# A four-layer attention kernel on one core: a new issue order, with key-value sums spread, the last key block in halves, and halo copies on GpSimd

## The chip, the core and the metric

The kernel runs on one core of a Trainium2 chip. A core has a matrix engine (TensorE, PE in the profile; its weight loads are listed as PEld), a vector engine (VectorE, DVE), a scalar engine (ScalarE, ACT), a general engine (GpSimd, POOL) and an engine that here only issues transfers (SyncE, SP). Each engine takes its instructions in the order of its own queue and waits on semaphores for the others. Data lies in SBUF, matrix products land in PSUM in eight banks of 128x512 fp32.

The metric is the device time of one execution in microseconds. Five runs of the kernel before gave a median of 334.54 us, from 333.26 to 336.47.

## The reference

Four layers, A, B, A, B, on x of 2048 rows by 512, 32 heads of 16. Each adds its result to x after a layer norm.

```python
def _A_ref(x, wqkv, w_phi, wo):
    pq = einsum("bhsd,hdf->bhsf", q, w_phi)          # the same for k
    phi_q = concatenate([softmax(pq), softmax(-pq)])  # the same for k
    kv = einsum("bhsf,bhsd->bhfd", phi_k, v)
    z  = einsum("bhsf->bhf", phi_k)
    o = einsum("bhqf,bhfd->bhqd", phi_q, kv) / (einsum("bhqf,bhf->bhq", phi_q, z) + 1e-6)
    return o @ wo
def _B_ref(x, wqkv, wo):
    # each row attends to 8 rows of its own past, 2 apart
    logits = einsum("bhsd,bhswd->bhsw", q, kg) * scale   # masked before row 0
    o = einsum("bhsw,bhswd->bhsd", softmax(logits), vg)
    return o @ wo
x = x + _A_ref(ln(x)); x = x + _B_ref(ln(x)); x = x + _A_ref(ln(x)); x = x + _B_ref(ln(x))
```

## The kernel before

The 2048 rows are four blocks (0 to 3) of 512; L is 0 for the first A and B layer and 1 for the second pair. Work is cut into steps, and a step issues a few instructions on one engine. The stages, with their lines in the profile:

- `s_a1` (A layer, keys and values of a block): projections L575 and L587, two exponentials of the keys on ACT L581, a tree of additions over 16 features on DVE L608 to L621 for four tiles at a time, the reciprocal on ACT L627 and L628, the normalising multiply on DVE L633, and the key-value sums L650. One sum step is for one tile of 128 rows: 16 small matmuls of 64 columns that add to one PSUM bank for the whole layer. Sixteen such steps make a layer's sums.
- `s_a2` (queries): projection L680, exponentials L688, their sums L696, logarithm and exponential for the reciprocal L702 and L703.
- `s_akv`: when all sums are in, eviction (through the helper `copy`: L184 is DVE, L186 is ACT), four transposes L726, and the masked copies ZM and R, L735 and L739. Nothing of `s_a3` can start earlier.
- `s_a3`: denominators L764, L772, L775, L778, L779, L783. Then, for blocks 0 and 1, the factor is spread over partitions by small matmuls L790 and multiplied into the query features on DVE straight from PSUM, L796. Blocks 2 and 3 go by way of DRAM, L803 and L810, with the multiply L814.
- `s_a4`: outputs L855, then `s_out`: output projection L511, the residual either as one more matmul L514 with an eviction on ACT L521, or as an addition on DVE L524; the squares L531 and `s_norm` for the next layer (L421 to L460), with transposes on PE (L453) or by a transfer (L444).
- `s_b1` (B layer): projections L879 of Q, K and V. K and V have 16 columns of halo in front: the last 16 columns of the block before. K's are copied on DVE (L905), V's go out to a small tile and in again on ACT (L921, L917). Block 0 has zeros, written by POOL (L909, L913). V is then copied by transfers on SP (L931) into Vg, in shifted form, 16 transfers per block.
- `s_b2`: products of queries and windows of keys on DVE, L960, one per quarter; sums of them by L967; exponentials L974, denominators L983, L988, L990, and probabilities L995.
- `s_b3`: products with the values on DVE L1020, summed by L1027, evicted by `copy`, and `s_out` again. In the last layer, `s_out` stores x (L535).
- `s_flag`: a check that no sum overflowed (L1048 to L1065); each engine loads the flag (L1072) and branches on it to a general version of the kernel, or past it.

The order is written out by hand. `_ORDER` is a list of base-36 numbers; each names one list of steps of a stage on one engine, and issues the next step of it. The queues of PE, DVE, ACT and SP follow this order, while POOL was left to the recording layer. `_CHOICE` has a digit for every step that may run on DVE (1) or ACT (0), and `_SLOTS` the buffer of each tile, for `big`, `med`, `t2` and PSUM tiles. A tile waits for the last reader of the tile that had its buffer.

## Time and profile before

| | us |
|---|---|
| median of the runs | 334.54 |
| the profiled execution | 332.56 |
| its span, first to last instruction | 330.8 |
| PEld busy | 149.8 |
| ACT busy | 281.2 |
| POOL busy | 5.8 |
| key-value sums L650, 512 matmuls, busy | 8.3 |
| L960, 32 instructions on DVE, busy | 72.2 |
| L1020, 32 instructions on DVE, busy | 71.7 |

Busy time of an engine is the time covered by its instructions; a matmul's end is modelled, so PE's is an upper value. In a line of the timeline stand the start, the time covered, the engine, the line of the kernel, the operation, output and inputs, shapes, and the count; the bracket gives the idle time of the engine just before and what ended it. "issue" is time in which the engine waited for nothing that the profile shows. The clock that was granted to PE was 0.995 of full speed over the execution.

### The profile page before, as it was taken

The page shows a single profiled execution, that of the slowest core. Times are in us where ns is not written, and L with a number is a line of the kernel's source. Part 1 is how long each engine was busy: PE and PEld are TensorE (multiplying, and loading weights), DVE is VectorE, ACT ScalarE, POOL GpSimd, SP SyncE. Part 2 cuts the span into 40 slices and gives each one's busy share as a digit, 9 for nine tenths or more (in the row PEclk, how much of TensorE's full clock was granted, in tenths as well). Part 3 has the DMA queues.
Part 4 walks back from the last instruction along what each step waited for, and adds up shares of the span by engine and source line. Part 5 has one row for each costly group of instructions (what it writes and reads, how often), then busy time and mean ns, then how long its engine had stood idle before and what let it go on. Part 6 is the DMA issues. An engine that isn't in the chain of part 4 may idle for free.

```text
span 330.8 us, 7975 instructions
## 1 busy us (share of the span) xinstructions
PE 310.8 (94%) x3189; PEld 149.8 (45%) x3189; DVE 300.4 (91%) x422; ACT 281.2 (85%) x644; POOL 5.8 (2%) x32
## 2 busy tenths in 40 slices
PE   8999997999999999999999999789999999997883
PEld 4645446545444444444444455643544444442321
DVE  4899995798899899999999999498999999999993
ACT  4999996899998898999999999788799998685630
POOL 4000000000000000000000000000000000000000
PEclk9999999999999999999999999999999999999997
DMA  7980000004399999794990300013469988689915
GB/s 211 322 232 3 0 0 4 4 14 124 80 157 112 181 132 173 126 141 105 159 133 13 63 1 2 4 40 101 108 91 159 123 162 157 139 142 155 186 54 168
DMA packets 37325, 35.42 MB, mean 107 GB/s; under 512 B 22944, under 2 KB 32160, under 8 KB 37280
## 3 DMA queue, kind: packets, MB, share of 16 engines
q1 hardware_dynamic: 36752, 34.81, 56.2%
q8 instruction: 27, 0.44, 0.6%
q14 instruction: 18, 0.15, 0.2%
q10 hardware_dynamic: 528, 0.02, 0.1%
HBM read 10.50 MB, written 2.36 MB: 39 GB/s over the span
## 4 chain that ended last, share of the span: by engine, by line
PE 66%; DVE 13%; ACT 11%; DMA 4%; issue 3%; SPq 0%; DVEq 0%; ACTq 0%
PE ps L879 19%; PE ps L511 13%; PE ps L575 6%; PE ps L587 6%; PE ps L680 5%; DMA xnT<-xn 4%; PE ps L967 3%; DVE Eq L796 3%; DVE prod L960 3%; PE ps L1027 3%; ACT oT L186 2%; DVE Ek L633 2%; PE ps L281 2%; ACT sqd L531 2%; PE ps L453 2%
## 5 line engine op out<-in xcount | busy, mean ns | idle before, releaser
L879 PE MATMUL ps<-xnT,WB 128*128 128x512 bf16 x384 | 88.5, 380 | 1.2 <-ACT V L186 0.7
L960 DVE TENSOR_TENSOR prod<-QT,K 128x4096 bf16<-128x4096 bf16 x32 | 72.2, 2287 | 1.1 <-ACT K L186 0.9
L1020 DVE TENSOR_TENSOR pav<-PT,Vg 128x4096 bf16<-128x4096 bf16 x32 | 71.7, 2288 | 0.9 <-PE ps L967 0.4
L879 PEld LDWEIGHTS <-WB 128*128 128x128 bf16 x384 | 42.2, 114 | 44.8 <-issue 7.8
L511 PEld LDWEIGHTS <-oT 128*128 128x128 bf16 x256 | 23.7, 98 | 31.9 <-ACT oT L186 4.1
L186 ACT CAST oT<-ps 128x512 bf16<-128x512 f32 x57 | 31.4, 603 | 6.4 <-PE ps L1027 5.3
L688 ACT ACTIVATE Eq<-ps 128x512 bf16<-128x512 f32 x64 | 35.0, 614 | 1.2 <-PE ps L680 1.1
L581 ACT ACTIVATE Ek<-ps 128x512 bf16<-128x512 f32 x64 | 34.2, 628 | 0.0
L511 PE MATMUL ps<-WoA,oT 128*128 128x512 bf16 x128 | 31.2, 380 | 1.4 <-ACT oT L186 1.4
L680 PE MATMUL ps<-xnT,WA 128*128 128x512 bf16 x128 | 31.0, 380 | 1.0 <-issue 0.8
L511 PE MATMUL ps<-WoB,oT 128*128 128x512 bf16 x128 | 31.5, 379 | 0.0
L587 PE MATMUL ps<-WA,xnT 128*128 128x512 bf16 x128 | 30.7, 379 | 0.0
L575 PE MATMUL ps<-WA,xnT 128*128 128x512 bf16 x128 | 30.0, 379 | 0.4 <-DMA xnT<-xn 0.4
L531 ACT ACTIVATE sqd<-x 128x512 bf16<-128x512 bf16 x48 | 30.0, 635 | 0.3
L524 DVE SCALAR_TENSOR_TENSOR x<-ps,x 128x512 bf16<-128x512 f32 x36 | 23.5, 686 | 1.0 <-PE ps L511 0.6
L521 ACT ACTIVATE x<-ps 128x512 bf16<-128x512 f32 x28 | 16.4, 597 | 8.0 <-PE ps L514 7.6
L439 ACT ACTIVATE xn<-x,nmr,rstd 128x512 bf16<-128x512 bf16 x27 | 21.4, 821 | 2.0 <-DVE nmr L428 2.0
L186 ACT CAST QT<-ps 128x512 bf16<-128x512 f32 x30 | 17.3, 593 | 3.6 <-issue 2.5
L796 DVE TENSOR_TENSOR Eq<-ps,Eq 128x512 bf16<-128x512 f32 x32 | 19.8, 684 | 0.1
L186 ACT CAST V<-ps 128x512 bf16<-128x512 f32 x31 | 17.5, 602 | 2.4 <-PE ps L879 2.4
L186 ACT CAST K<-ps 128x512 bf16<-128x512 f32 x30 | 17.7, 595 | 2.1 <-PE ps L879 1.8
L1027 PE MATMUL ps<-pav,indAV 128*32 128x512 bf16 x256 | 17.0, 382 | 2.6 <-DVE pav L1020 2.6
(126 smaller groups left out, 406.9 us busy)
## 6 DMA issues: line engine op xcount, KB each, us to landing
Vg<-V SPq DMA_DIRECT2D x128, 131.5 KB, 4.8
Prho<-rd SPq DMA_DIRECT2D x8, 512.0 KB
out_dram<-x SPq DMA_DIRECT2D x8, 256.0 KB, 3.9
x<-in_A_x_dram SPq DMA_DIRECT2D x3, 512.0 KB, 7.1
WB<-in_B_wqkv_dram SPq DMA_DIRECT2D x3, 512.0 KB, 10.3
wraw<-in_A_wqkv_dram SPq DMA_DIRECT2D x4, 256.0 KB
x<-in_A_x_dram SPq DMA_DIRECT2D x4, 128.0 KB, 4.4
WA<-in_A_wqkv_dram SPq DMA_DIRECT2D x1, 512.0 KB
```

The source lines that it names most:

```text
L186: self.nc.scalar.copy(out=out, in_=in_)
L511: nc.tensor.matmul(y[:], lhsT=oT[:, c, t * P:(t + 1) * P], rhs=Wo()[:, c, :], start=(c == 0), stop=(c == NB - 1 and not onpe))
L531: nc.scalar.activation(out=sqd[:], in_=xb[:, t, :], func=ACT.Square, accum_out=T["ss"][:, t:t + 1])
L575: nc.tensor.matmul(pk[:], lhsT=xnT[:, t, k, :], rhs=self.WA[:, k, D:2 * D], start=(k == 0), stop=(k == NB - 1))
L581: nc.scalar.activation(out=T["E"][:, t, s, :], in_=T["k", t][:], func=ACT.Exp, scale=1.0 - 2.0 * s)
L587: nc.tensor.matmul(pv[:], lhsT=xnT[:, t, k, :], rhs=self.WA[:, k, 2 * D:3 * D], start=(k == 0), stop=(k == NB - 1))
L680: nc.tensor.matmul(pq[:], lhsT=self.WA[:, k, hb * P:(hb + 1) * P], rhs=xnT[:, :, k, :], start=(k == 0), stop=(k == NB - 1))
L688: nc.scalar.activation(out=self.Eq[L, b][s][:, :, hb, :], in_=T[hb][:].rearrange("p (t i) -> p t i", t=4), func=ACT.Exp, scale=1.0 - 2.0 * s)
L796: nc.vector.tensor_tensor(out=ev, in0=T["pb", s][t][:].rearrange("p (a i) -> p a i", a=NB), in1=ev, op=ALU.mult)
L879: nc.tensor.matmul(pp[:], lhsT=self.WB[:, k, i * D + c:(i + 1) * D:NB], rhs=xnT[:, :, k, :], start=(k == 0), stop=(k == NB - 1))
L960: nc.vector.tensor_tensor(out=pr[:], in0=QT[:, c:c + 1, :].to_broadcast([P, NW, TB]), in1=win, op=ALU.mult)
L1020: nc.vector.tensor_tensor(out=pv[:], in0=PT[:].unsqueeze(1).to_broadcast([P, NB, 2, TB]), in1=vw, op=ALU.mult)
```

## The change

The order, the choices and the slots are replaced as a whole. In the new order the key-value sums of a layer no longer stand in one run: in layer 0 eight steps, then four value projections, then the other eight; in layer 1 eight steps, then seven projections, then the other eight. The feature normalisation of key block 3 is issued for two tiles at a time (`half_k`). The halo copies go to POOL, and POOL's queue now follows the order as well. The eviction of the products from PSUM in `s_a3` becomes a choice for each tile: multiplied straight from PSUM, or copied to SBUF by ACT first (7 of 32 are). The eviction of the key-value sums is on DVE. The load of the flag may be issued within the order, 12 steps after the flag is computed; nine steps follow that point in the new order. `split`, which would cut the last steps in two, is empty.

```diff
 _OPT = {
-    "rho_act": (),
-    "half_k": (),
+    "half_k": ((0, 3), (1, 3)),
     "half_ln": (),
+    "split": (),
     "warm": 14,
+    "flag_lag": 12,
 }
-_ORDERED = {_E.PE, _E.DVE, _E.Activation, _E.SP}
+_ORDERED = {_E.PE, _E.DVE, _E.Activation, _E.SP, _E.Pool}
 _ORDER = """
-0 0 0 8 i 9 i i i i i i i i i i i i i 2t j o k j l a b p 3 3 o q 1x 1x 1z 27 r s 2 1q 1y 1x 1x 20 t 1r 0 t 1x
...
+d5 0 bh 4i 9 8 i i i i i i i a i i i 0 i i i i 0 d f g c j k o p j 3 t l h 1x 3 1x 0 2 o 2i q r b t m n 1y 1q
...
-        def mulp(s, t):
+        def mulp(s, t, direct):
             ev = self.Eq[L, b][s][:, t, :, :]
-            nc.vector.tensor_tensor(out=ev, in0=T["pb", s][t][:].rearrange("p (a i) -> p a i", a=NB), in1=ev,
-                                    op=ALU.mult)
+            src = T["pb", s][t] if direct else T["bs", s, t]
+            nc.vector.tensor_tensor(out=ev, in0=src[:].rearrange("p (a i) -> p a i", a=NB), in1=ev, op=ALU.mult)
...
-        def bev(s, t, dve):
...
+        def bev(s, t, direct):
+            if direct:
+                self.slot("t2")
+            else:
+                T["bs", s, t] = self.t2([TB], "bs")
+                nc.scalar.copy(out=T["bs", s, t][:], in_=T["pb", s][t][:])
...
-            nc.vector.tensor_copy(out=self.K[L, b][:, :, 0:16], in_=self.K[L, b - 1][:, :, TB:KVW])
+            nc.gpsimd.tensor_copy(out=self.K[L, b][:, :, 0:16], in_=self.K[L, b - 1][:, :, TB:KVW])
...
-            nc.scalar.copy(out=T["V"][:, :, 0:16], in_=self.vh[L, b - 1][:])
+            nc.gpsimd.tensor_copy(out=T["V"][:, :, 0:16], in_=self.vh[L, b - 1][:])
...
-            nc.scalar.copy(out=self.vh[L, b][:], in_=T["V"][:, :, TB:KVW])
+            nc.gpsimd.tensor_copy(out=self.vh[L, b][:], in_=T["V"][:, :, TB:KVW])
...
-            add(st + "v", "ACT", vhalo_in)
+            add(st + "v", "POOL", vhalo_in)
...
-            add(st + "k", "DVE", halo)
+            add(st + "kh", "POOL", halo)
         if b < 3:
-            add(st + "v", "ACT", vhalo_out)
+            add(st + "v", "POOL", vhalo_out)
...
         for w in _ORDER.split():
             key = self.names[int(w, 36)]
             i = n.get(key, 0)
             n[key] = i + 1
             self.threads[key][i]()
+            if key == "flag.DVE" and i == 1:
+                left = _OPT["flag_lag"]
+            if left is not None:
+                left -= 1
+                if left == 0:
+                    self.redo = self.flag()
+        if left is None or left > 0:
+            self.redo = self.flag()
...
-        redo = fast.flag()
+        redo = fast.redo
```

The amounts of work change little: VectorE issues 405 instructions up to the flag in place of 394, ScalarE 547 in place of 555, TensorE one matmul less, GpSimd 18 copies more.

## The prediction

> **What bounds the kernel now.** I read the busy shares first, then busy time by stretch of the span, then the order of time inside the stretches that have idle time.

> ```profile
> PE 310.8 (94%) x3189; PEld 149.8 (45%) x3189; DVE 300.4 (91%) x422; ACT 281.2 (85%) x644; POOL 5.8 (2%) x32
> ```

> ```profile
> 50.00:68.00 18.00, 15.64 (x557) 10.16 (x556) 12.65 (x28) 13.53 (x31) 0.54 (x2) 1.00 0.01 4
> ...
> 208.00:224.00 16.00, 12.96 (x435) 7.60 (x427) 11.31 (x26) 12.50 (x29) 0.00 (x0) 1.00 0.11 27
> ```

> ```profile
> 215.65:320.24 104.59, 97.47 (x873) 44.28 (x876) 102.23 (x109) 83.65 (x199) 0.15 (x1) 1.00 0.71 128
> 61.44:206.35 144.91, 143.67 (x1211) 66.16 (x1211) 138.75 (x188) 137.63 (x324) 1.46 (x5) 1.00 0.60 98
> ```

> The columns after the length are busy us of PE, weight loads, DVE, ACT and POOL. Four parts show. From 61 to 206 us PE is the bound (143.67 of 144.91 busy). From 215.65, where the last layer's feature products begin, to 320.24, where the last attention product ends, DVE is the bound (102.23 of 104.59). After 320.24 a tail runs out. Between lie two hand-overs, at the end of the key-value sums of each layer (50 to 61, 206 to 216), in which every engine idles: in the windows around them PE idles 2.36 and 3.04 us, DVE 5.35 and 4.69. A gain must come out of these two, the tail, or DVE's queue after 215.65; more work for ACT or POOL costs nothing by itself.

> ```profile
> 50.30 2.91 PE L650 MATMUL ps<-Ek,vaug 128*33 128x64 bf16 x176
> 54.40 1.35 PE L650 MATMUL ps<-Ek,vaug 128*33 128x64 bf16 x80 [1.20 <-issue]
> 55.68 0.63 PE L696 MATMUL ps<-Eq,indS 128*32 128x128 bf16 x32
> 56.42 0.40 PE L726 MATMUL ps<-ident,kvT 128*128 128x128 bf16 x4
> 56.75 0.35 PE L696 MATMUL ps<-Eq,indS 128*32 128x128 bf16 x12
> 57.85 0.46 PE L696 MATMUL ps<-Eq,indS 128*32 128x128 bf16 x20 [0.75 <-issue]
> ```

> ```profile
> 209.74 0.29 PE L696 MATMUL ps<-Eq,indS 128*32 128x128 bf16 x6
> 210.95 0.57 PE L696 MATMUL ps<-Eq,indS 128*32 128x128 bf16 x26 [0.93 <-issue]
> ...
> 214.68 0.60 PE L680 MATMUL ps<-xnT,WA 128*128 128x512 bf16 x2 [0.84 <-issue]
> ```

> Four times PE stops with no engine to wait for: 1.20, 0.75, 0.93 and 0.84 us, 3.72 together. Count between the stops: 80+32+4+12 = 128 matmuls in layer 0, 26+4+32+64+2 = 128 in layer 1 (the rows between are the transposes and L696, L764). With a weight load each that is 256 instructions. In 50 to 60 us the transfers hold one queue alone, three packets of some 16 KB:

> ```profile
> q8 instruction: 3, 0.05, 1.9%
> ```

> So PE takes in instructions in blocks of 256, and a new block was there 54.40 to 57.85 = 3.45 us after the one before, or 210.95 to 214.68 = 3.73. 128 pairs of L650 take 128 x 16.3 ns (8.3 us over 512) = 2.1 us and run dry; 128 matmuls of 512 columns take 27 us and never do.

> [...]

> **The change, part by part.** All steps are made against the profiled execution, 332.56 us, of which the span is 330.8. The shown runs have median 334.54; I take the difference over to it unchanged.

> 1. *Layer 0, sums spread.* Decoded, the new PE order is: eight key-value steps of 16 matmuls, four value projections (16 x 216 ns = 3.5 us), four steps, four steps, a Q projection (0.86), the transposes, a Q projection, then denominators (32 small), sums (32), denominators (32), a Q projection. Cut in blocks of 128 from the same count (the start has as many), the shortest holds 3.9 us of work (104 x 16.3 ns, 16 small, 8 x 216), above 3.45. Both stops should go: -1.95. The Q projection before the transposes covers the eviction of the sums (0.58 on ACT before, 0.69 on DVE now). Of PE's idle 2.36 I take **-2.2**. PE bounds what follows, so all of it counts.

> 2. *Last key block in halves* (L608 to L633 for block 3). DVE work: the four-tile multiply is 2.287, halves are 2 x 1.22 (the 128x2048 row L814), tree and reciprocal halves add about 0.3 a level by the next smaller rows: +1.6 a layer, ACT +0.35. That lies where PE is the bound and DVE has 144.91 - 138.75 = 6.2 us free. In return, only two sum steps (32 x 16.3 = 0.5) instead of four (1.1) follow the last multiply: -0.6 on the chain.

> 3. *Layer 1 hand-over.* Before: the last multiply ends at 208.64, the first product L796 begins at 215.65, 7.0 us. After, link by link with the durations of that stretch: two sum steps 0.6, L696 0.72 (covers the eviction), transposes 0.46, the other L696 0.72 (covers L735 and L739), L764 0.6, L772/775 0.75, L778/779 0.8, L783 0.45, L790 0.46: 5.6. Stops come on top. One block of 128 still has only 2.1 us of work and the next 3.5, but steps in the first wait for the two last multiplies anyway. Between no stop (-1.4) and both (+0.4) I choose 0.4 us of stops: **-1.0**.

> 4. *After the first product of layer 1 (DVE).* Ahead of the last product L1020: three more residual adds (3 x 0.69), three K halos less (3 x 0.176), four L796 products from SBUF in place of PSUM (0.684 to 0.425, the same shape in bf16, L616): +2.06 - 0.53 - 1.04 = +0.5. The four take ACT 4 x 0.6, which has 20.9 us free here. Three more of them in layer 0 are hidden likewise; they put an ACT link before a product, but other products are queued between.

> 5. *Tail.*

> ```profile
> 306.94 13.30 DVE L1020 TENSOR_TENSOR pav<-PT,Vg 128x4096 bf16<-128x4096 bf16 x6
> ...
> 325.13 0.69 DVE L524 SCALAR_TENSOR_TENSOR x<-ps,x 128x512 bf16<-128x512 f32 x1 [0.30 <-PE ps L511]
> ```

> From 320.24 to 325.82 is 5.58. Before, L1027 for the last two products ran together after PE had finished an output projection, and one projection adds x on PE. New: L1027 0.66, eviction 0.63, the 13 matmuls left (13 x 0.216 + 0.16 = 2.97), add 0.74: 5.0, so -0.6. With part 4: **-0.1**. The 5.0 us from 325.82 to 330.8 stay: store, its landing (3.9 median), the closing barrier.

> 6. *Flag register.* The load is put 12 steps after the flag is known, but only nine steps follow in the new order, so it is issued at the end: in each engine's queue it stays last. **0**: that part does not do what it says.

> 7. *Halos on POOL.* 18 copies leave ACT (12 x 0.26, not the bound) and DVE (counted). A K halo waits for ACT's evictions of the earlier block; the first L960 of the block waits for it. A V halo stands before 16 Vg copies on SP (131.5 KB, 4.8 us to land each), behind which normalised transposes queue. The trace has no POOL copy. Nearest rows: POOL's memset of the same 128x64 shape, 0.15 (L913), and of a strided one, 0.39 to 0.48 (L596). [...] I take **+0.4**, nearer the rows; ends 0 and 4.3.

> 8. *Start and the rest of the order.* Both evictions of the first folded weight are now on ACT (1.0 each, one was 0.69 on DVE): **+0.3**, ends 0 and 0.6. DVE's named waits after 215.65 sum to 1.6 (L428 0.6, L543 0.5, L524 0.3, L960 0.2); the new order has large products queued ahead of some: **-0.3**, ends +0.5 and -1.6. PE's two waits for transposed x (0.47, 0.43) may stay or go.

> Sum: -2.2 - 1.0 - 0.1 + 0.4 + 0.3 - 0.3 = -2.9: 329.7 for the profiled execution, **331.6** for the median.

> **Rivals.**
> (a) *The waits elsewhere shrink too*: both transposed-x waits (0.9), DVE's 1.6 and all stops of layer 1 (0.4) go, POOL costs nothing (0.4): about 3 more, 328.6. For it: the order is new everywhere. Against: PE and DVE have under 2% idle there. Chance 0.22.
> (b) *The gain is not collected*: stops move to layer 1 (+1.4 against my choice) and DVE's queue takes back 0.8: 333.8, no measurable change. For it: the short block of 2.1 us. Chance 0.13.
> [...] Chance 0.08.
> My forecast has 0.57.

> **Numbers.** Range 328.0 to 335.2: it takes in (a) for the most part, (b), and my own -1.5 to -5 from the bounds above, and leaves out most of (c). 0.5% (1.67 us) is about what can be told from no change here. Faster: 0.57 less a little, (a), a little of (b): 0.79; same 0.13; slower 0.08.

> **What will show it.** Right: no issue stop over 0.3 us at layer 0's key-value sums, first L796 of layer 1 near 212 to 213 us, register loads last on every queue, DVE still full from there to the last L1020, and under 5.2 us from it to the last add. Wrong: stops inside the spread sums; POOL copies lasting over 0.5 us or DVE gaps of that size beside them; PE idle between 61 and 206 us that makes up for layer 0; or a later first L796 although the stops are gone.

## The result and the profile after

Timed side by side on the same chip, the changed kernel took 332.51 us (median of 26, 330.60 to 335.75) and the kernel before 334.4 us. The ratio is 0.9939, with a 95% interval from 0.9923 to 0.9956: about 2.0 us less. The ratios leave out slow executions, one of the 26 here, and so differ a little from the ratio of the medians. A second series of the same pair gave 0.9951 (0.9927 to 0.9976). So the change is a gain, within the range, and about two thirds of the 2.9 us that the forecast summed up.

The profiled execution took 331.27 us with a span of 329.55 (332.56 and 330.84 before), 1.29 us less. The busy shares show nothing of it:

```profile
PE 311.5 (95%) x3188; PEld 150.6 (46%) x3188; DVE 302.1 (92%) x435; ACT 278.7 (85%) x634; POOL 28.4 (9%) x50
```

DVE has 1.7 us more work and POOL 22.6 more. The windows of the two hand-overs, and then the two long stretches between the marks of the prediction (columns as there):

```profile
50.00:68.00 18.00, 17.20 (x431) 9.59 (x429) 14.14 (x29) 15.67 (x36) 0.00 (x0) 1.00 0.02 4
208.00:224.00 16.00, 14.07 (x355) 7.24 (x353) 14.03 (x32) 14.60 (x36) 0.00 (x0) 1.00 0.24 64
```

```profile
211.93:319.29 107.36, 99.12 (x875) 45.21 (x874) 103.10 (x111) 84.84 (x193) 12.56 (x9) 0.98 0.79 129
58.62:206.32 147.70, 146.88 (x1384) 69.57 (x1384) 141.00 (x191) 137.43 (x323) 10.57 (x12) 1.00 0.51 96
```

PE's idle time fell from 2.36 to 0.80 us and from 3.04 to 1.93 in the hand-overs. In the last stretch, DVE's work grew from 102.23 to 103.10 us and its idle time from 2.36 to 4.26. Cut at the same marks, the two executions read (in us):

| stretch | before | after | predicted change | measured |
|---|---|---|---|---|
| to the first product of layer 0, L796, now L812 | 61.44 | 58.62 | -1.9 | -2.82 |
| to the last multiply of layer 1's keys, L633, now L647 | 147.20 | 147.70 | 0 | +0.50 |
| hand-over to the first L812 of layer 1 | 7.01 | 5.61 | -1.0 | -1.40 |
| to the last product with the values, L1020, now L1036 | 104.59 | 107.36 | +0.6 | +2.77 |
| tail, to the last addition to x, L524, now L529 | 5.58 | 5.44 | -0.6 | -0.14 |
| to the end of the span | 5.02 | 4.82 | 0 | -0.20 |

The rows add up to the 1.29 us between these two executions, not to the 2.0 us between the medians; 0.7 us of the gain stands in no trace.

Both hand-overs gave more than predicted. One stretch gave 2.8 us back, and not all along: from the first product of layer 1's B layer (L960, now L974) to the last L1036 both kernels take 79.3 us. The loss lies in the 28.11 us before that product (25.31 before).

The sums themselves, on PE's timeline, in layer 0 and then in layer 1:

```profile
45.27 2.05 PE L664 MATMUL ps<-Ek,vaug 128*33 128x64 bf16 x128
47.25 3.63 PE L601 MATMUL ps<-WA,xnT 128*128 128x512 bf16 x16
50.81 2.19 PE L664 MATMUL ps<-Ek,vaug 128*33 128x64 bf16 x128
...
205.00 2.05 PE L664 MATMUL ps<-Ek,vaug 128*33 128x64 bf16 x128
...
207.83 0.40 PE L740 MATMUL ps<-ident,kvT 128*128 128x128 bf16 x4 [0.23 <-DVE kvT L187]
```

No stop by issue is left in either hand-over: four stops of 3.72 us are gone. But PE's timeline has one in a new place, and DVE's, below it, is held by it:

```profile
223.97 0.39 PE L516 MATMUL ps<-WoA,oT 128*128 128x512 bf16 x1
225.97 1.67 PE L516 MATMUL ps<-WoA,oT 128*128 128x512 bf16 x7 [1.61 <-issue]
```

```profile
224.75 0.41 DVE L797 TENSOR_TENSOR rho<-rS,Ds 128x256 bf16<-128x256 f32 x1
226.81 0.69 DVE L529 SCALAR_TENSOR_TENSOR x<-ps,x 128x512 bf16<-128x512 f32 x1 [1.64 <-PE ps L516]
```

Counted in PE's instructions, the place lies a whole number of blocks (16 x 256) behind the place of the 1.20 us stop of the kernel before. But PE took 7.5 and 6.0 us for the two blocks ahead of it (210.5 to 218.0 and 218.0 to 224.0 us), more than the 3.45 to 3.73 us in which a block arrived. Small matmuls alone don't explain it. The transfers do more: PE passed the place before, at 217.99 us, and the queue's own timeline has the broadcast reads of block 2 issued just ahead of that:

```profile
215.87 1.38 SPq L825 DMA_DIRECT2D Prho<-rd  x2
```

All that moved from 218.3 to 223.2 us, and then from 223.2 to 224.6 (queue, packets, MB, share of the transfer engines):

```profile
q1 hardware_dynamic: 162, 0.63, 48.3%
```

```profile
q1 hardware_dynamic: 41, 0.17, 47.7%
q8 instruction: 1, 0.02, 5.6%
```

For five microseconds only the two reads of 512 KB move, but for eight packets of 4 bytes. Then, at 223.22, comes the one packet of instructions, and 1.5 us after its end PE goes on. The packet does not wait for the reads' end: 199 of their 256 packets have started by then, and the last ends at 226.2. Elsewhere such a packet mostly starts 0.5 to 1.7 us after PE has passed a place. In the kernel before, PE passed the place at 220.77 and the packet began at 221.56, just as these reads got going:

```profile
220.15 1.37 SPq L810 DMA_DIRECT2D Prho<-rd  x2
```

This gave the theory that the experiments tested first.

### The profile page after: what moved, and what is told of

Its sections match the earlier page's. It is cut to its first block, busy times and chain, and to the rows that moved or that the text cites. A ratio compares the mean times of both kernels' runs of the same rounds, so it can differ in the third digit from the quotient of the medians.

```text
span 329.6 us, 8014 instructions
## 1 busy us (share of the span) xinstructions
PE 311.5 (95%) x3188; PEld 150.6 (46%) x3188; DVE 302.1 (92%) x435; ACT 278.7 (85%) x634; POOL 28.4 (9%) x50
## 3 DMA queue, kind: packets, MB, share of 16 engines
HBM read 10.50 MB, written 2.36 MB: 39 GB/s over the span
## 4 chain that ended last, share of the span: by engine, by line
PE 62%; DVE 11%; DMA 11%; ACT 6%; SPq 5%; issue 4%; DVEq 0%; ACTq 0%
PE ps L516 12%; PE ps L893 11%; PE ps L601 9%; PE ps L589 8%; PE ps L694 7%; DMA Vg<-V 7%; DVE prod L974 5%; SPq L945 4%; PE ps L664 2%; DVE pav L1036 2%; PE ps L1045 2%; DMA xnT<-xn 2%; PE ps L456 2%; ACT xn L442 2%; PE ps L981 2%
## 5 line engine op out<-in xcount | busy, mean ns | idle before, releaser
L893 PE MATMUL ps<-xnT,WB 128*128 128x512 bf16 x384 | 87.4, 380 | 0.0
L974 DVE TENSOR_TENSOR prod<-QT,K 128x4096 bf16<-128x4096 bf16 x32 | 72.4, 2288 | 0.3 <-ACT K L189 0.3
L1036 DVE TENSOR_TENSOR pav<-PT,Vg 128x4096 bf16<-128x4096 bf16 x32 | 71.6, 2292 | 0.4
L516 PEld LDWEIGHTS <-oT 128*128 128x128 bf16 x256 | 24.0, 98 | 35.3 <-issue 5.8
L189 ACT CAST oT<-ps 128x512 bf16<-128x512 f32 x56 | 30.7, 600 | 8.0 <-PE ps L1045 6.4
L516 PE MATMUL ps<-WoB,oT 128*128 128x512 bf16 x128 | 33.3, 387 | 0.6 <-ACT oT L189 0.6
L595 ACT ACTIVATE Ek<-ps 128x512 bf16<-128x512 f32 x64 | 33.1, 624 | 0.0
L516 PE MATMUL ps<-WoA,oT 128*128 128x512 bf16 x128 | 30.6, 380 | 1.6 <-issue 1.6
L529 DVE SCALAR_TENSOR_TENSOR x<-ps,x 128x512 bf16<-128x512 f32 x37 | 24.4, 688 | 2.8 <-PE ps L516 2.2
L935 POOL COPY vh<-V 128x64 bf16<-128x64 bf16 x6 | 8.9, 1478 | 147.2 <-ACT V L189 140.4
L442 ACT ACTIVATE xn<-x,nmr,rstd 128x512 bf16<-128x512 bf16 x24 | 19.0, 822 | 1.5 <-DVE nmr L431 1.5
L647 DVE TENSOR_TENSOR Ek<-Ek,rk 128x4096 bf16<-128x4096 bf16 (+1 forms) x10 | 18.6, 1860 | 0.5 <-ACT rk L642 0.5
## 6 DMA issues: line engine op xcount, KB each, us to landing
Vg<-V SPq DMA_DIRECT2D x128, 131.5 KB, 5.4
```

The costliest lines, as they stand in the source:

```text
L189: self.nc.scalar.copy(out=out, in_=in_)
L442: nc.scalar.activation(out=xn, in_=xt, func=ACT.Identity, scale=rstd, bias=sh)
L516: nc.tensor.matmul(y[:], lhsT=oT[:, c, t * P:(t + 1) * P], rhs=Wo()[:, c, :], start=(c == 0), stop=(c == NB - 1 and not onpe))
L595: nc.scalar.activation(out=T["E"][:, t, s, :], in_=T["k", t][:], func=ACT.Exp, scale=1.0 - 2.0 * s)
L893: nc.tensor.matmul(pp[:], lhsT=self.WB[:, k, i * D + c:(i + 1) * D:NB], rhs=xnT[:, :, k, :], start=(k == 0), stop=(k == NB - 1))
L974: nc.vector.tensor_tensor(out=pr[:], in0=QT[:, c:c + 1, :].to_broadcast([P, NW, TB]), in1=win, op=ALU.mult)
```

## The experiments

Theory T1: the stop at 226 us is a block of instructions that waits behind the broadcast reads. Rivals: the order of the outputs costs that time anyway (T2), or the place has nothing to do with it (T3). Then the parts of the change were undone one by one, and one was done alone in the kernel before.

All stretches below are in us from the profiled execution of each run; "hand-over" is the part of the second stretch from the last multiply of layer 1 to its first L812. "Half clock" is how long TensorE was granted 0.50 ahead of the last addition to x. Each ratio is to the kernel before as timed in the same series. There were four series behind the first: shift64, shift48, group and halo_back (chip 4); again, shift_free, halo_back2 and fullk (chip 1); late_read, flag_early and before_spread (chip 9); late_again (chip 15). Only on chip 1 was the changed kernel itself timed beside its variants.

| kernel | ratio to the kernel before (95%) | first projection | to first product, layer 0 | to that of layer 1 | hand-over | to first product of B | to last L1036 | tail | half clock |
|---|---|---|---|---|---|---|---|---|---|
| before | 1 | 12.52 | 48.93 | 154.21 | 7.01 | 25.31 | 79.28 | 5.59 | 0 |
| changed | 0.9939 (0.9923 to 0.9956) | 12.27 | 46.36 | 153.31 | 5.60 | 28.11 | 79.25 | 5.44 | 3.4 |
| changed, again | 0.9951 (0.9927 to 0.9976) | 12.28 | 46.35 | 153.38 | 5.61 | 27.83 | 79.24 | 5.75 | 3.4 |
| shift64 | 1.0040 (1.0019 to 1.0062) | 13.39 | 46.34 | 156.34 | 6.44 | 26.59 | 79.24 | 5.80 | 3.4 |
| shift48 | 1.0009 (0.9984 to 1.0034) | 13.89 | 46.35 | 156.13 | 6.62 | 26.58 | 79.24 | 6.85 | 6.8 |
| shift_free | 0.9991 (0.9971 to 1.0011) | 12.98 | 46.35 | 154.88 | 6.29 | 26.58 | 79.25 | 6.32 | 6.8 |
| late_read | 0.9951 (0.9920 to 0.9981) | 12.67 | 46.34 | 153.16 | 5.61 | 26.64 | 79.27 | 6.72 | 6.8 |
| late_again | 0.9933 (0.9912 to 0.9954) | 13.13 | 46.35 | 153.17 | 5.61 | 26.64 | 79.27 | 6.94 | 6.8 |
| group | 1.0012 (0.9988 to 1.0037) | 11.92 | 47.20 | 155.81 | 6.46 | 29.92 | 79.25 | 5.75 | 3.4 + 3.4 |
| fullk | 1.0067 (1.0043 to 1.0091) | 12.86 | 50.24 | 155.42 | 6.04 | 27.97 | 78.97 | 6.64 | 3.4 + 6.8 |
| halo_back | 1.0163 (1.0117 to 1.0209) | 11.56 | 46.56 | 155.23 | 5.61 | 28.22 | 86.58 | 5.75 | 3 x 3.4 |
| halo_back2 | 0.9980 (0.9951 to 1.0008) | 12.84 | 46.34 | 153.46 | 5.62 | 27.92 | 79.66 | 5.74 | 3.4 |
| flag_early | 0.9911 (0.9877 to 0.9945) | 11.64 | 46.33 | 154.35 | 5.61 | 28.65 | 79.24 | 7.42 | 6.8 |
| before_spread | 0.9982 (0.9962 to 1.0003) | 12.55 | 48.42 | 154.03 | 6.83 | 25.27 | 79.27 | 5.59 | 0 |

### The place of the blocks shifted: shift64, shift48, shift_free

```diff
         def warm():
             nc.tensor.matmul(self.warm_ps[:], lhsT=self.kvT[:, 0:P], rhs=self.kvT[:], start=True, stop=True)
+            self.nwarm = getattr(self, "nwarm", 0) + 1
+            if self.nwarm == 6:
+                for _ in range(64):
+                    nc.tensor.matmul(self.warm_ps[0:32, 0:16], lhsT=self.kvT[:, 0:32], rhs=self.kvT[:, 0:16],
+                                     start=True, stop=True)
```

shift48 has 48 instead of 64. In shift_free, 70 of the tiny matmuls stand in the place of warming matmuls 6 to 11.

> The changed kernel with 64 tiny matmuls (32x16 outputs, 128 instructions of PE with their weight loads) more among the first warming ones; nothing else moves. They shift by half a block the places at which PE needs its next 256 instructions: in the trace of the changed kernel the place just before layer 1's broadcast reads goes from 217.99 us (its fetch waited until the two reads of 512 KB were through, 223.2) to 213.7 us, 2 us before the reads are issued, and the next to 219.4. T1 (the issue stop of 1.61 us at 226 us is a block of instructions queued behind the broadcast reads): no issue stop above 0.3 us between 212 and 240 us, the products of layer 1's B start 1.6 us or more earlier after the first multiply of L812, time -1.6 us (-1.0 to -3.0) against the changed kernel, near 330.5. T2 (the new order of the outputs takes the gain back, the stop only stands where DVE or ACT would have been late anyway): the stop goes but the time stays within 0.5 us. T3 (the stop has nothing to do with the place in the instruction stream): a stop of 1.0 to 2.0 us stays at about 226 us.

> As the one with 64, but with 48 tiny matmuls (96 instructions): the place at which PE asks for its next block goes to 215.8 us, the time at which the broadcast reads are issued, and the next place, where that block is needed, to 220.0 us. T1: if the fetch falls behind the reads, PE stops from 220.0 to about 225.5, so 4 to 6 us of issue stop there and +3 to +5 us in the time against the changed kernel; if it slips in ahead of them, no stop and the time of the kernel with 64. T2: within 0.5 us of the changed kernel, whatever the stop. T3: the stop of 1.0 to 2.0 us stays at about 226 us, time within 0.5 us.

> The shift by 128 instructions of PE without its price: 70 tiny matmuls stand in the place of 6 of the 14 warming ones (128 instructions more in all), so that the first projection starts near 12.3 us instead of 13.4. T1: no issue stop above 0.3 us from 212 to 245 us, the stretch from the first L812 of layer 1 to the first product of its B is 26.0 to 27.0 us instead of 28.1, time -1.5 us (-0.8 to -2.5) against the changed kernel run beside it. T2 (the order takes it back): stretch shorter but time within 0.5 us. T3: no change in stretch or time.

In all three the stop at the outputs is gone, and the stretch to the first product of B is 26.6 us in place of 27.8 to 28.1. (The expectation of shift64 has the fetch wait until the reads were through; by the packets above it began before that.) PE's timeline of shift_free, in which L516 is L522 and L778 is L784:

```profile
210.90 0.63 PE L784 MATMUL ps<-Eq,ZM 128*32 128x128 bf16 x32 [0.49 <-DVE R L759]
...
226.24 2.15 PE L522 MATMUL ps<-WoA,oT 128*128 128x512 bf16 x7
```

The same seven matmuls, cut apart in the changed kernel, are one group without a stop. So T3 falls, and T1 gets its stretch. But the expectation of a shorter time was wrong: shift_free is 1.35 us longer than the changed kernel beside it. The first row shows one reason. The same shift carries another place into the hand-over of layer 1, where the matmuls are small: a fetch began at 208.30 and ended at 209.62, and PE went on at 210.90, 1.28 us after that end; the hand-over takes 6.29 us against 5.61. The bracket names R, but R cannot be what L784 waited for: in the changed kernel the same matmuls start at 208.62, while R is still being written (208.47 to 208.89). The rest is the start (0.7 later), a wait of DVE for layer 0's own broadcast read (1.38 against 0.53 us), and the tail (0.6). In shift48 the fetch began at 219.12, before the reads were issued at 221.76, for the whole kernel runs later there: it slipped ahead of them, the second of the two outcomes set down, with a stop of 0.83 us in the hand-over instead. The shift moves stops; it does not remove them. By their ratios shift64 is about 3 us and shift48 about 2 us longer than the changed kernel. In their traces the first projection starts 1.1 and 1.6 us later, the hand-over takes 0.8 and 1.0 us more, and DVE waits 2.54 and 2.24 us for layer 0's broadcast read.

### The changed kernel once more: again

> The changed kernel itself, once more, on the chip of these runs: the measure for the other three, as the first four runs showed layer 0's second broadcast read landing 2 us later than in the trace of the changed kernel. Ratio to the kernel before 0.994 (0.990 to 0.998). If the late landing belongs to the chip and not to the edits, DVE waits 2 to 2.5 us for it at about 100 us here too; if it belongs to the edits, 0.4 us as in the first trace.

The ratio is the one expected. DVE waits 0.53 us for layer 0's second broadcast read, and 0.15 us in halo_back2, 0.71 in fullk and 1.38 in shift_free. The first four runs, with 2.00 to 2.54 us, were all on chip 4, on which the changed kernel was not run, so whether the late landing belongs to that chip or varies between executions stays open. Up to 2.5 us of a trace's second stretch, and as much of these four runs' times, can be due to it and not to the edit.

### The read held back: late_read, late_again

```diff
         def rdb(s):
             rd = self.RD[L, b]
             T["P", s] = pr = self.med([4, NB, P], "Prho")
...
+            if (L, b, s) == (1, 2, 1):
+                nc.gpsimd.tensor_copy(out=pr[:, 0, 0, 0:1], in_=self.oT["B1", 0][:, 2, 0:1])
             nc.sync.dma_start(out=pr[:].rearrange("p t a i -> p (t a i)"), in_=src)
```

In `_ORDER` the three transfer steps of this block (the write and the two reads) also stand further ahead, at the same place among SP's transfers, and two `med` buffers trade places.

> The changed kernel with nothing moved on PE; the second of the two broadcast reads of layer 1's block 2 (512 KB) is held back until the eviction of block 0's third output on DVE (218.7 us) by a copy of one column on GpSimd into its tile; it is used at 228.7 us. PE's place to ask for instructions stays at 218.0 us. T1 (the fetch of 16 KB waits behind all reads already issued): it now stands behind one read instead of two and starts near 219.5 to 220.5 us instead of 223, so the issue stop at 225.8 us (1.3 to 1.6 us) is below 0.3 us, the stretch from the first L812 to the first product of B is 26.4 to 27.2 us instead of 27.8 to 28.1, time -1.0 us (-0.3 to -1.8) against the changed kernel, ratio to the kernel before 0.990 to 0.993. T3 (not the reads): the stop stays at 1.3 us or more, ratio 0.994 to 0.996. Loss: if the second read lands after 227 us, DVE waits for it and the time is that of the changed kernel or more.

The queue's timeline and PE's:

```profile
216.10 3.73 SPq L827 DMA_DIRECT2D Prho<-rd  x2
```

```profile
224.20 2.15 PE L516 MATMUL ps<-WoA,oT 128*128 128x512 bf16 x7
```

With nothing moved on PE, the stop is gone here too. The packet of instructions began at 221.54 instead of 223.22: later than expected (219.5 to 220.5), but 2.7 us ahead of the place where it is needed. 137 of the reads' 256 packets had started by then, so it came right behind the first read. Two edits that share nothing but the order of a fetch and a read remove the same stop, so T1 is shown. The stop cost 1.2 to 1.5 us of the 2.8 in that stretch. The last product ends at 318.08 although the kernel started 0.4 later, against 319.09 and 319.29.

Yet the time did not follow. The ratio of 0.9951 can't be told from the changed kernel's, and in the trace the tail grew by about what was gained, to 6.72 us. So T2 is wrong about the stretch, but its sign, a time that stays within 0.5 us, came true: no run shows the stop's removal as time gained in the whole kernel. A second series asked whether that was chance.

> The kernel with the second read held back, once more, to see whether it beats the changed kernel in time. In its first trace the issue stop was gone and the last product of layer 1's B (L1038 there) ended 1.0 us earlier than in the changed kernel's second trace although its first projection began 0.4 us later, but its median ratio was 0.9951 (0.992 to 0.998), no better than 0.9939 and 0.9951 of the changed kernel; TensorE's granted clock was 0.50 from 311 to 317 us in it, and the last output projections came late. If the lower clock there was that one run's: ratio 0.990 to 0.993. If the clock is lowered in that stretch in this kernel as a rule: ratio 0.993 to 0.996 again, and 0.50 between 310 and 317 us in this trace too.

It was not. The clock was at half again for 6.8 us, the tail was 6.94, and the ratio 0.9933. The window from 314 to 316 us of the kernel before, of the changed kernel and of late_read (the third number from the end is the granted clock):

```profile
314.00:316.00 2.00, 0.41 (x12) 0.12 (x8) 2.00 (x2) 0.94 (x2) 0.00 (x0) 1.00 0.78 269
```

```profile
314.00:316.00 2.00, 2.00 (x7) 0.78 (x6) 2.00 (x2) 0.51 (x2) 0.00 (x0) 0.61 1.09 316
```

```profile
314.00:316.00 2.00, 2.00 (x6) 0.71 (x5) 2.00 (x2) 1.07 (x2) 0.00 (x0) 0.50 1.09 383
```

In the new order, PE waits 0.62, 1.59 and 1.59 us for three products of the last block (308 to 312.7 us) and then gets half the clock for 3.4 us, in late_read for 6.8, while output projections are due. The last of these waits in the changed kernel:

```profile
312.74 1.04 PE L1045 MATMUL ps<-pav,indAV 128*32 128x512 bf16 x8 [1.59 <-DVE pav L1036]
```

The kernel before waits 0.99 and 1.59 us there and keeps its clock. In late_read the sums of the last product start at 319.75, 1.67 us after it, since a projection is still in front of them; in the changed kernel 0.40 us after it. So the gain of 1.2 to 1.5 us was lost within the last 20 us. What is shown is that the longer half clock and the longer tail come together, and not only here: in the table the tail is 5.4 to 5.8 us behind 0 or 3.4 us at half clock, and 6.3 to 7.4 behind 6.8. No run held the clock up to see the tail shrink, and the timed executions leave the cause open. A mean granted clock under 0.988 is listed for 25 of the 42 executions of the changed kernel that its two ratios use, and for 4 of 174 of the kernel before in the four later series. In the changed kernel their medians lie 1.25 and 0.75 us above those of the executions with 0.9925 or more (332.95 against 331.70, 332.14 against 331.39). But in late_again they lie 0.85 us below (331.63 for fifteen, 332.48 for five). This mean also takes in the clock behind the last matmul, so it does not say where the clock was low.

### The sums put together again: group

The sum steps of blocks 0 and 1, but for the very first, go behind the wide projections, in `_ORDER` alone. Written with the names of the steps (kv is a sum step, mv a value projection), layer 0 is:

```diff
-... a1_00 kv kv kv kv, a1_01 kv kv kv kv ..., a1_03v mv mv mv mv, ... a1_02 kv ...
+... a1_00 kv ..., a1_03v mv mv mv mv, a1_00 kv kv kv, a1_01 kv kv kv kv, ... a1_02 kv ...
```

> The changed kernel with the key-value sums put together again: in each of the two A layers seven sum steps (blocks 0 and 1 of the layer) are issued only after the wide projections that stood behind them, so that 15 of 16 sum steps follow one another on PE. Prediction's step 1 (a run of more than 128 small matmuls outruns the supply of instructions): issue stops of 0.75 to 1.3 us come back in the sums of layer 0 and of layer 1, the first L812 of layer 0 is 1 to 3 us later (near 60 to 61.5 us) and that of layer 1 1 to 3 us later (213 to 215), time +2 us (+1 to +4). Rival (the gain at layer 0 came from the other places of the steps, not from the spread): no stop above 0.3 us, time within 0.7 us of the changed kernel.

The time is 0.6 to 0.7% above the changed kernel's two ratios, +2.0 to +2.4 us, the size expected. But the changed kernel was not run on this chip, and this trace, too, has DVE waiting 2.08 us for layer 0's broadcast read (0.40 and 0.53 in the changed kernel's), so not all of it need be the sums'. PE's timeline in layer 1:

```profile
205.51 3.68 PE L664 MATMUL ps<-Ek,vaug 128*33 128x64 bf16 x240
...
210.33 0.57 PE L710 MATMUL ps<-Eq,indS 128*32 128x128 bf16 x28 [0.97 <-issue]
```

The stop is back, and the hand-over of layer 1 is 0.85 us longer. In layer 0 no stop came back: PE waits 0.58 us for an eviction on ACT within the sums, and the first product is 0.84 later relative to the start, less than expected. The stop at the outputs is there as well (1.75 us), and right behind it the clock is at half for 3.4 us, which goes with this one trace's stretch of 29.92; the execution is the slowest of its runs (336.78 us, median 334.35).

### The last block whole again: fullk

```diff
-            for f in (t8, t4, t2, t1):
-                add(st, "DVE", f, t, m)
-            add(st, "ACT", rr, t, m)
-            add(st, "DVE", mul, t, m)
+            for f in (t8, t4, t2, t1):
+                add(st, "DVE", whole, f, t, m)
+            add(st, "ACT", whole, rr, t, m)
+            add(st, "DVE", whole, mul, t, m)
```

`whole` does nothing for the first half, and all four tiles for the second. In `_ORDER` the block's first sum step comes behind the multiply.

> The changed kernel with the last key block of each A layer normalised whole again: the steps of its first half do nothing, those of the second do all four tiles, and its first sum step comes after the multiply. Prediction's step 2 (the halves save 0.6 us a layer on the way from the last multiply to the last sum, and cost 1.6 us of DVE that is hidden): DVE busy 3 us less, the last multiply ends 0.7 to 1.5 us later in both layers, first L812 of either layer 0.5 to 1.5 us later, time +1.0 us (+0.4 to +2.0). Rival (the DVE work of the halves isn't hidden in layer 1): time -0.5 to -1.5 us.

It is 1.16% longer than the changed kernel beside it, 3.9 us: twice the upper end expected. PE's timeline in layer 0:

```profile
55.12 1.89 PE L664 MATMUL ps<-Ek,vaug 128*33 128x64 bf16 x64 [1.94 <-DVE Ek L647]
```

PE waits for the last multiply, which ends at 55.07 against 52.31 us. The new order puts the last two multiplies close to the sums. With halves the last one takes 1.22 us; whole it takes 2.29, and the tree ahead of it waits 1.33 us until ACT has all four tiles. So the run prices a whole block in an order that was written for halves. A part of this trace's 3.9 us in layer 0 is the clock, at half for 3.4 us from 54.5: the multiply ends 2.2 us later, counted from the first projection, and 1.7 us are added behind it. The traced execution is also longer than the median of its runs (338.86 against 336.93 us).

### The spread alone, in the kernel before: before_spread

```diff
-... a2_00 mq mq mq, ... a1_00 kv kv kv kv, a1_01 kv kv kv kv ... a1_02 kv ...
+... a1_00 kv kv kv kv, a1_01 kv kv kv kv, a2_00 mq mq mq ... a1_02 kv ...
```

This is layer 0 (mq is a query projection); the PSUM buffers of the moved steps change with them.

> The kernel before with one part of the change alone: three query projections (12 wide matmuls) of layer 0 and two (8) of layer 1 are issued after the first eight key-value sum steps instead of ahead of them; the rest of the order is the old one. Prediction's step 1: the issue stops of layer 0 (1.20 and 0.75 us) and of layer 1 (0.93 and 0.84 us) fall to 0.4 us or less in all for each layer, first multiply of L796 1.0 to 2.2 us earlier in layer 0, time -2 us (-0.8 to -3.5) against the kernel before. Rival (the spread pays only together with the halves, since the last sum waits for the last multiply at 52.3 us): the stops go, but the last sums end less than 0.7 us earlier and the time is within 0.7 us of the kernel before. Rival (the stops move on): as many us of stops stand elsewhere, no gain.

```profile
48.33 0.38 PE L643 MATMUL ps<-kvT 128*128 128x512 bf16 x1 [0.74 <-ACT vaug L186]
48.64 2.05 PE L650 MATMUL ps<-Ek,vaug 128*33 128x64 bf16 x128
50.62 2.77 PE L680 MATMUL ps<-xnT,WA 128*128 128x512 bf16 x12
53.31 2.05 PE L650 MATMUL ps<-Ek,vaug 128*33 128x64 bf16 x128
...
57.38 0.46 PE L696 MATMUL ps<-Eq,indS 128*32 128x128 bf16 x20 [0.66 <-issue]
```

The stops fall from 1.95 to 0.66 us in layer 0 and from 1.77 to 1.13 in layer 1. The last sums end at 55.36 instead of 55.74, and the time falls by 0.6 us, with an interval that reaches no change. These are the numbers of the first rival, but not its reason. The last 128 sums start at 53.31 us, 1.0 us after the last multiply ends (52.30) and right behind the projections, so they do not wait for it. The time of the first stop went elsewhere: with the projections moved behind them, the first sums come earlier, and PE waits 0.74 us in front of them for an eviction on ACT; 0.66 us of the second stop stayed. So the spread alone pays little in this order; that it pays because of the halves is not shown.

### The halo copies: halo_back, halo_back2

```diff
-            nc.gpsimd.tensor_copy(out=self.K[L, b][:, :, 0:16], in_=self.K[L, b - 1][:, :, TB:KVW])
+            nc.vector.tensor_copy(out=self.K[L, b][:, :, 0:16], in_=self.K[L, b - 1][:, :, TB:KVW])
...
-            nc.gpsimd.tensor_copy(out=T["V"][:, :, 0:16], in_=self.vh[L, b - 1][:])
+            nc.scalar.copy(out=T["V"][:, :, 0:16], in_=self.vh[L, b - 1][:])
...
-            nc.gpsimd.tensor_copy(out=self.vh[L, b][:], in_=T["V"][:, :, TB:KVW])
+            nc.scalar.copy(out=self.vh[L, b][:], in_=T["V"][:, :, TB:KVW])
```

> The changed kernel with its three kinds of halo copies back where they were: K's halo on DVE, V's halo in and out on ACT, at the same places of the order. Prediction's step (copies on GpSimd cost 0.4 us net, copies lengthened and now and then late for who waits for them): -0.2 us (-0.8 to +0.3). Rival (they cost nothing and free 3 copies of 0.16 us on DVE and 6 of 0.2 to 0.3 us on ACT): +0.3 to +0.8 us. [...]

The expectations missed: it is 2.1 to 2.2% above the changed kernel's ratios, 7 us. DVE's timeline tells why:

```profile
266.25 0.18 DVE L919 COPY K<-K 128x64 bf16<-128x64 bf16 x1 [2.91 <-ACT K L189]
...
281.94 0.18 DVE L919 COPY K<-K 128x64 bf16<-128x64 bf16 x1 [4.32 <-ACT K L189]
```

The place that is free on GpSimd is not on DVE. There the copy waits for an eviction on ACT, and the products queue behind it: 2.91 + 4.32 = 7.2 us of waits, in a stretch that is 7.3 us longer. The run does not price the copies, but what their place is worth. So the K copy was moved to just ahead of its block's first product:

```diff
         def prod(c):
             K, QT = self.K[L, b], self.QT[L, b]
+            if b and c == 0:
+                nc.vector.tensor_copy(out=K[:, :, 0:16], in_=self.K[L, b - 1][:, :, TB:KVW])
```

> The halo copies back on the engines they came from, but K's copy issued on DVE only when the block's first product is issued, where its source has long been evicted (in the run before it stood where GpSimd has it, and DVE waited there 2.9 and 4.3 us for an eviction on ACT); V's on ACT as in that run. Prediction's step (0.4 us lost by GpSimd): -0.2 us (-0.8 to +0.3) against the changed kernel. Rival H (the gain of GpSimd is that its waits hold nobody else's queue; where the copy doesn't wait it is worth only its 0.16 to 0.3 us): +0.2 to +0.8 us, not the +6 us of the run before. If it is +3 us or more, the copies on ACT wait too, and a wait of more than 0.5 us stands in front of them on ACT.

The stretch to the last L1036 is 0.42 us longer than in the changed kernel, near the three copies of 0.18 us on DVE. The time, +0.3% (+1.0 us), is within the two intervals. Rival H fits the stretch: GpSimd saves DVE its copies and, at the places that this order gives them, 7 us of waiting in the wrong queue. No loss by GpSimd shows. What the copies do on GpSimd in the changed kernel:

```profile
100.93 0.26 POOL L931 COPY V<-vh 128x64 bf16<-128x64 bf16 x1
...
113.80 2.18 POOL L919 COPY K<-K 128x64 bf16<-128x64 bf16 x1 [5.67 <-ACT xn L442]
```

```profile
L974 DVE TENSOR_TENSOR prod<-QT,K 128x4096 bf16<-128x4096 bf16 x32 | 72.4, 2288 | 0.3 <-ACT K L189 0.3
```

Eleven of the 18 copies take 1.3 to 2.2 us; each of them runs beside one product on DVE and ends 0.1 us after it. One takes 0.70 beside the multiply L1009, and six take 0.24 to 0.28, beside L529, L440 or L187. The product, with a mean of 2288 ns, keeps its 2287 ns of before. So where the two ran side by side, the copy on GpSimd lasted longer and the product did not.

### The flag register early: flag_early

```diff
-    "flag_lag": 12,
+    "flag_lag": 3,
```

> The changed kernel with flag_lag 3 instead of 12: the load of the flag into a register is now really issued ahead of what is left, two steps after the decision, with seven steps behind it (on PE, ACT and SP). Prediction's step 6 (the loads cost nothing where they are last): 0 us against the changed kernel. If a load that is ahead takes something off the end: -0.3 to -1.0 us. If it holds its engine until the flag is written, and PE's or ACT's last output steps wait behind it: +0.5 to +3 us, with the last addition to x later by as much.

```profile
325.01 1.89 PE L516 MATMUL ps<-WoB,oT 128*128 128x512 bf16 x8 [1.05 <-DVE fl L1087]
```

The load holds PE for 1.05 us in front of the last eight matmuls, and the tail is 7.42 us, against 6.3 to 6.9 in the other traces with 6.8 us at half clock. But the ratio, from only six timed runs, is 0.9911, lower than the changed kernel's; the intervals overlap. The trace shows a loss in the tail, the times show none, so whether the early load costs or gains anything is open.

## Why the prediction was right, and where not

It said 331.6 us for the median where 332.5 was measured, and faster. Its sum of -2.9 was made for the traced execution, which gained 1.29; the medians gained 2.0. That the total came so near owes something to luck, for errors of both signs stand in it. By its own steps:

1. *Layer 0, -2.2*: -2.57 from the first projection on. The stops are as it counted, in blocks of 256, and they are gone. But the prediction gave the whole gain to the spread. The spread alone, in the order before, brought 0.5 us to this stretch and 0.6 to the kernel, for a wait on ACT took the place of a stop; undone in the new order it cost 0.84 in layer 0 without any stop there. How the gain divides between the spread, the halves and the other places of the steps is not shown. Over the whole execution, PE's stops by issue came to 3.7 us in the kernel before and 1.6 in the changed one.
2. *Last block in halves, -0.6 a layer, hidden otherwise*: the added work looks hidden (PE is busy for 146.88 of 147.70 us between the hand-overs), but whole blocks in this order cost 3.9 us, not 1.2. The prediction looked at what follows the last multiply, not at the two multiplies close together that the order puts there.
3. *Hand-over of layer 1, -1.0*: -1.40. The sum of the links was right (5.6 us predicted, 5.61 measured); the 0.4 us of stops allowed for did not come.
4. *DVE's work in the last stretch, +0.5*: +0.87.
5. *Tail, -0.6*: -0.14, and 5.44 us is over the 5.2 that it had named as a sign. The sums of the last product started 0.40 us late behind a projection, after the 3.4 us at half clock that no step of the prediction held.
6. *Flag register, 0*: the loads stayed last, as read from the order; forced early, the load showed a loss in the trace and none in the times.
7. *Halo copies, +0.4*: about 0. The copies do last over 0.5 us, which the prediction had named as a sign against it, but DVE has no gap beside them. No run shows the +0.4 or its end of 4.3, nor the slower kernel to which the prediction gave a chance of 0.08: beside the copies the products on DVE take 2288 ns, as before (2287), while eleven of the copies last 1.3 to 2.2 us.
8. *Start, +0.3*: the first projection came 0.25 us earlier; over the traces above it starts between 11.56 and 13.89 us, so nothing can be said of this term. *The rest of the order, -0.3, ends +0.5 and -1.6*: the term that failed. DVE's idle time in the last stretch grew by 1.90 us, more than the end of +0.5. Most of that is the stop of 1.61 us for the block of instructions behind the broadcast reads, which cost 1.2 to 1.5: rival (b) had stops moving on and DVE's queue taking back the gain, but placed the stops in layer 1's sums and took them for small matmuls. It could have been looked for by asking what each moved transfer runs beside.

So the first stretch and the hand-over together were 1.3 us too careful, and the last stretch and the tail 2.6 too hopeful; 0.5 us in the long middle stretch, and 0.2 at the end, had no step.

## What to carry to other kernels

Count the instructions of a stage as well as its work: here a block of 256 instructions, 128 of the matmuls L650 with their weight loads, held 2.1 us of work, and a block arrived 3.45 to 3.73 us after the one before. Where a block runs dry like that, try spreading it, but look at what PE waits for next, since the spread alone paid 0.6 us where 3.7 us of stops stood. A transfer can hold up an engine that doesn't use it, as 1 MB of reads cost PE a stop of 1.61 us here: see what is issued in the few us before the engine needs its next block. Holding back the part that is used last took that stop away here, though the time did not fall. A part undone in an order that was written around it prices the order too: the three undone here cost about 2, 4 and 7 us, where the whole change brings 2. When an operation is moved to an idle engine, ask what its place is worth as well as its duration: in DVE's queue two K copies of 0.18 us waited 7.2 us with the products behind them (halo_back), and on GpSimd their waits held nobody else (79.25 us for the stretch, against 86.58).

## What the runs showed of the hardware that was not expected

A fetch of 16 KB for PE waited behind reads that were issued before it: in the changed kernel it began 5.2 us after PE passed the place (217.99 to 223.22 us) behind 1 MB of reads, and in late_read, with half of them held back, 3.3 us after, instead of the 0.5 to 1.7 of most others. It began with 199 and 137 of the 256 packets of the reads started, so not behind all of them.
